# An FFT mixer and an MLP mixer in one kernel: four weight sums moved to GpSimd, and the folds of two early batches taken in other pieces at other steps

## The chip, the cores and the metric

The kernel runs on one core of a Trainium2 chip. The metric is the device time of one execution in microseconds (us); the kernel before has a median of 597.24 us over 6 executions, from 595.39 to 599.65. The engines are called by the names of the profile: PE is TensorE (PEld its weight load), DVE is VectorE, ACT is ScalarE, POOL is GpSimd, SP is SyncE.

## The reference

The input x has 8 batches of 3008 rows and 256 features. First the real part of a two-dimensional Fourier transform over rows and features is taken, then an MLP mixer: a token part over the rows and a channel part over the features, each with a relu and a residual.

```python
X = np.fft.fft(np.fft.fft(x, axis=1), axis=2).real        # (8, 3008, 256)
h = np.maximum(X.transpose(0, 2, 1) @ w_tok1, 0.0) @ w_tok2
u = X + h.transpose(0, 2, 1)
out = u + np.maximum(u @ w_ch1, 0.0) @ w_ch2              # w_ch1 256x1536, w_ch2 1536x256
```

## The kernel before

Everything is computed in f16 with f32 sums in PSUM. All loops are unrolled, and each engine works through its instructions in the order in which the program writes them; semaphores between the engines are put in from the tiles that they share. There is no planner at run time: the order is the written one, and lists of small numbers (`plan`, `own_plan`, `early_plan`, `fold_plan`) say how many pieces of a generator are taken at which place.

**Setup (lines 104 to 980)** makes the tables of the transform, loads the weights and does batch 0's transform. Loads that turn f32 into f16 are issued by POOL: x of batch 0, the token weights, `wc1` and `wc2` (the channel weights; `wc2` is tile `wc` in the profile), then x of batch 1. After the loads POOL copies most of the second token weights into aligned rows (`align_w2`, lines 976 to 978; eight copies w2p<-w2s at L305).

**A batch is 24 steps.** For each of 6 chunks `c` of 512 rows there are 4 steps `s`; step number `sub = 4 * c + s`. A step holds, in this order: three of the 12 tiles of the first channel product with relu on ACT (`mm1`, L773, L776), pieces of the batch's own transform that are still open (`own`), pieces of the next batch's transform (`nxt`), a quarter of the second channel product of the chunk before (`mm2`, L817), and block sums on DVE (`now`, `block_sums`, L790). Batch 0's step 0 starts at 32.18 us, batch 1's at 102.88.

**The second channel product** is done on 2x2 blocks with seven block products instead of eight. For that it needs sums of blocks of the activations (`block_sums`, tiles `c` and `sb`) for each chunk, and once four sums of blocks of the weights: `wst`, 128x768 each, made by `weight_sums` (lines 230 to 235) on DVE at step 3 of batch 0. Their first reader is PE in step 5 (`wst[:, 0]`, then `wst[:, 1]`), then steps 6 and 7. ACT copies partial results (`m`, L822), DVE adds them up (`osb`, L799), POOL adds the residual `rt` (L799) after filling one edge column of it (`edges`, L794), and SP issues the output. `rt` is the transposed `ut`, by DMA transposes on SP's queue (`turn_u`, L753).

**The transform of a batch** begins with `fold` on DVE (lines 451 to 474): x (`xp`) plus its mirrored rows (`xm`, loaded by an indirect gather), then even and odd parts in `eo`. It has four quarters of the 17 rows of tile, and each quarter has three pieces: add into xp (L463), even part (L467), odd part (L472). The first piece carries two short column adds more (L461, L462), the eleventh a copy and a memset (L469, L470). `front` then multiplies `eo` with tables (`inner` L518, `outer` L527, L583) into `z`, `z` into `w` (L596, L597, L599), and `w` into the token part: `tok1` (L613), `third` (L645, with ACT's `qs` L648 and DVE's two `yt` L652), and per chunk two products `pu` (L730) whose sum with `yt` DVE writes into `ut` (L738).

**Buffers.** `xp`, `xm`, `eo` have one buffer: `load_x(b)` waits until the fold of the batch before has read xp for the last time. `load_x` is four copies and two gathers on POOL (L163, L153). PSUM has three rings: tag "mm" (3 buffers, `mm1`), "o2" (2, `mm2`), "f" (3, the transform).

**What is taken where, before.** fold(1) is taken in batch 0 by `early_plan`: 2, 0, 2, 2, 3, 2, 1 pieces at steps 5 to 11; behind it at step 11 comes `load_x(2)`. fold(2) is taken by `fold_plan`: two pieces each at steps 16, 17, 20 and 21 of batch 0 and at steps 0 and 1 of batch 1; behind it at step 1 comes `load_x(3)`. fold(3) begins at step 9 of batch 1. `own_plan[1]` gives the open pieces of batch 1's transform at its own steps: first third(2), then `ut` of chunks 2 to 5 in halves.

Of the kernel before, what the change touches and what calls it, by code (L numbers as in the profile page):

```python
# [21 lines left out]
BB = 8  # L22
# [19 lines left out]
def kernel(  # L42
# [9 lines left out]
    nc = tc.nc  # L52
# [32 lines left out]
    def dram(t, offset, ap):  # L85
        return bass.AP(tensor=t, offset=offset, ap=ap)
# [8 lines left out]
    def ts(out_, in_, s1, op0, s2=None, op1=None, eng=nc.vector):  # L95
        if op1 is None:
            eng.tensor_scalar(out=out_, in0=in_, scalar1=s1, scalar2=None, op0=op0)
        else:
# [16 lines left out]
                      for n in ("tdu", "tdb", "altu"))  # L115
# [7 lines left out]
                                   in1=pcol[:], op0=AT.mult, op1=AT.add)  # L123
# [28 lines left out]
    def gather(out_, rows, index):  # L152
        nc.gpsimd.indirect_dma_start(  # L153
            out=out_, out_offset=None, in_=rows,
            in_offset=bass.IndirectOffsetOnAxis(ap=index, axis=0))

    def load_x(b):
        xp = xin.tile([KR, NR, D], FP16, tag="xp", name="xp")
        xm = xin.tile([KG, NR - 1, D], FP16, tag="xm", name="xm")
        for i in range(2):  # L160
            for q, n in ((0, 32), (32, NQ - 32)):
                p0 = i * NQ + q
                nc.gpsimd.dma_start(  # L163
                    out=xp[p0:p0 + n, :, :],
                    in_=dram(x_t, (b * S + 16 * i + 64 * q) * D,
                             [[64 * D, n], [1, NR * D]]))
        xmf = xm[:].rearrange("p t d -> p (t d)")
        for k in range(2):
            gather(xmf[:, 8 * D * k:8 * D * (k + 1)], x8, ix8[0:KG, b, k:k + 1])
        return xp, xm  # L170
# [5 lines left out]
    x_tiles = {0: load_x(0)}  # L176
# [51 lines left out]
    wst = const.tile([P, 4, HC, P], FP16, tag="wst")  # L228

    def weight_sums():  # L230
        b11, b12, b21, b22 = (wc2[:, HC * j:HC * j + HC, P * k:P * k + P]
                              for j in range(2) for k in range(2))
        for o, x, y, op in ((0, b12, b11, AT.subtract), (2, b22, b12, AT.subtract),
                            (1, wst[:, 2], b11, AT.add), (3, b21, wst[:, 1], AT.subtract)):
            nc.vector.tensor_tensor(out=wst[:, o], in0=x, in1=y, op=op)

    def swap_wc1(h):
        nc.sync.dma_start(out=wc1[1][:, h, :], in_=wc1[0][:, h, :])
# [64 lines left out]
    def copy(e, out_, in_):  # L303
        if e:
            (nc.vector, nc.gpsimd)[e - 1].tensor_copy(out=out_, in_=in_)  # L305
        else:
            nc.scalar.activation(out=out_, in_=in_, func=AFT.Copy)  # L307
# [12 lines left out]
        out=mp[:], in0=jrow[:, 0:64].unsqueeze(1).to_broadcast([P, NG, 64]),  # L320
# [123 lines left out]
    def align_w2(c, th, e):  # L444
        a = slice(8 * c, min(8 * c + 8, NQ))
        copy(e, w2p[:, th, :, a], w2v[:, th, :, a])
# [4 lines left out]
    def fold(b, engs):  # L451
        xp, xm = x_tiles.pop(b)
        eo = perb.tile([KR, NR, D], FP16, tag="eo", name="eo")
        state[b] = {"eo": eo}
        add, sub = AT.add, AT.subtract
        for s, (t0, t1) in enumerate(((13, 17), (9, 13), (5, 9), (1, 5))):
            tt = engs[s].tensor_tensor
            t = slice(t0, t1)
            rv = slice(16 - t0, 16 - t1 if t1 < 17 else None, -1)
            if s == 0:  # L460
                tt(out=xp[:, 1:NR, 0], in0=xp[:, 1:NR, 0], in1=xm[0:KR, ::-1, 0], op=add)  # L461
                tt(out=eo[:, :, 0], in0=xp[:, :, 0], in1=xp[:, :, 0], op=add)  # L462
            tt(out=xp[:, t, 1:D], in0=xp[:, t, 1:D], in1=xm[0:KR, rv, D - 1:0:-1], op=add)  # L463
            yield
            if t0 == 1:
                t = slice(0, t1)
            tt(out=eo[:, t, 1:129], in0=xp[:, t, 1:129], in1=xp[:, t, 255:127:-1], op=add)  # L467
            if t0 == 1:
                nc.vector.tensor_copy(out=nyq[:, 0:1], in_=eo[:, 0, P:P + 1])  # L469
                nc.vector.memset(eo[:, 0, P:P + 1], 0.0)  # L470
            yield
            tt(out=eo[:, t, 129:256], in0=xp[:, t, 1:128], in1=xp[:, t, 255:128:-1],  # L472
               op=sub)
            yield
# [284 lines left out]
    def plain(b, c):  # L759
        return (b, c) == (BB - 1, NCH - 1)  # L760

    def tiles(b, c):
        return 1 if c + 1 == NCH and b % 2 == 0 else 2
# [157 lines left out]
    def pair(b, c1):  # L921

        if b % 2 == 0 and b + 1 < BB:
            state["ch"] = work.tile([P, NCT, 64], FP16, tag="ch", name="ch")
            nc.vector.tensor_copy(out=state["ch"][:], in_=c1[:, :, CW - 128:CW - 64])
        elif b % 2:
            nc.vector.tensor_copy(out=c1[:, :, CW - 64:CW], in_=state["ch"][:])


    def take(g, n):  # L930
        for _ in range(n):
            next(g, None)
# [43 lines left out]
    for c in range(2, NCH):  # L976
        for th in range(2):
            align_w2(c, th, 2)
    early = fold(1, [nc.vector] * 4)
    setup.close()  # L980
    work = ctx.enter_context(tc.tile_pool(name="work", bufs=1))
# [2 lines left out]

    plan = [[0] * 10 + [2] * 10 + [1, 2, 2, 3]] + [[1] * 14 + [2, 1] * 4 + [1, 1]] * (BB - 1)
    own_plan = [[2, 1, 1, 1, 1, 1, 1, 0, 1, 1, 0, 0, 1, 1] + [0] * 10,
                [1, 1, 1, 0, 0, 1, 1, 0, 1, 1, 0, 0, 1, 1] + [0] * 10]
    own_plan += [[1, 1, 1, 0, 0, 1, 1, 0, 1, 1, 0, 0, 1, 1] + [0] * 10] * (BB - 2)
    early_plan = [0] * 5 + [2, 0, 2, 2, 3, 2, 1] + [0] * 12
    fold_plan = [[0] * 8 + [1, 2, 0, 0] * 4 for _ in range(BB)]  # L990
    fold_plan[0] = [0] * 16 + [2, 2, 0, 0, 2, 2, 0, 0]
    fold_plan[1] = [2, 2, 0, 0] + [0] * 4 + [0, 2, 0, 0] + [1, 2, 0, 0] * 2 + [2, 2, 0, 0]
    prev = None
    turned_u = {(0, 0): turn_u(0, 0)}
    for b in range(BB):
        nxt = front(b + 1) if b + 1 < BB else iter(())
        if b != 1:
            folds = fold(b + 2, [nc.vector] * 4) if b + 2 < BB else None
        for c in range(NCH):
            c1 = work.tile([P, NCT, CW], FP16, tag="c1", name="c1", bufs=2)  # L1000
            box = {"rt": turned_u.pop((b, c))}
            if not plain(b, c):
                box["sb"] = work.tile([P, 3, HC, D], FP16, tag="sb", name="sb", bufs=2)
            if c + 1 == NCH and b % 2:
                pair(b, c1)
            for s in range(4):
                sub = 4 * c + s
                n = plan[b][sub]
                mm1(b, c, c1, range(3 * s, 3 * s + 3))
                def now():  # L1010
                    which = 2 * (s % 2), 2 * (s % 2) + 1
                    if s >= 2 and not plain(b, c) and (b or c):
                        block_sums(c1, box["sb"], slice(0, 3), which, tiles(b, c))
                    elif s < 2 and prev is not None:
                        k = slice(3 if b or c > 1 else 0, HC)
                        block_sums(prev[2], pbox["sb"], k, which, tiles(*prev[0:2]))

                if s == 3:
                    now()
                take(own, own_plan[b][sub])  # L1020
                first = 0 if s % 2 else n // 2
                take(nxt, first)
                if s == 0:
                    now()
                if prev is not None:
                    mm2(*prev, s, pbox)
                if s in (1, 2):
                    now()
                take(nxt, n - first)
                if s == 2 and c + 1 < NCH:  # L1030
                    turned_u[b, c + 1] = turn_u(b, c + 1)
                if s == 3 and c + 1 == NCH and b + 1 < BB:
                    turned_u[b + 1, 0] = turn_u(b + 1, 0)
                if b == 0 and sub in (15, 17, 19, 21):
                    align_w2((sub - 15) // 4, (sub - 15) // 2 % 2, 0)
                if b == 0 and sub == 3:
                    weight_sums()
                    for h in range(2):
                        swap_wc1(h)
                if b == 0 and early_plan[sub]:  # L1040
                    take(early, early_plan[sub])
                    if sub == 11:
                        x_tiles[2] = load_x(2)
                if folds is not None and fold_plan[b][sub]:
                    take(folds, fold_plan[b][sub])
                    if b == 1 and sub == 1:
                        x_tiles[3] = load_x(3)
                        folds = fold(3, [nc.vector] * 4)
                if sub == 22 and b and b + 3 < BB:
                    x_tiles[b + 3] = load_x(b + 3)  # L1050
            if c + 1 == NCH and b % 2 == 0:
                pair(b, c1)
            prev, pbox = (b, c, c1), box
        own = nxt
# [32 lines left out]
```

## Time and profile before

| | us |
|---|---|
| median of 6 executions | 597.24 |
| the profiled execution | 596.69 |
| its span, first to last instruction | 594.9 |
| PE busy | 580.2 |
| DVE busy | 460.5 |
| ACT busy | 440.3 |
| POOL busy | 154.3 |
| PE waits listed, after 33 us | 0.2 (45.4), 0.3 (71.4), 1.2 (82.9) |
| x of batch 2: first issue, first DVE reader | 66.82, 82.07 |
| the four weight sums on DVE | 40.54 to 42.7 |

The profile is of one execution. A timeline row gives start and length in us, engine, line, operation, output <- inputs with their shapes, and in brackets how long the engine stood idle before it and for whom. A waits row gives who waited for whom, the total, the count and the longest. PE's ends are modelled; the rhythm of its starts is more exact. Intervals between starts are called pitch: an instruction overlaps the end of the one before, so a row's length is a little more than its pitch.

### The profile page before, as it was taken

How to read it: one execution, taken by the hardware profiler on the slowest of the kernel's cores; microseconds unless marked ns; L12 is line 12 of the kernel's file. 1: busy time of each engine (PE TensorE's matmuls, PEld its weight loads, DVE VectorE, ACT ScalarE, POOL GpSimd, SP SyncE). 2: the span in 40 equal slices, each digit the busy share in tenths (PEclk: the TensorE clock that was granted, in tenths of full speed). 3: DMA queues.
4: the chain of work that ended last, by engine and by line, in shares of the span. 5: the costliest groups of instructions: out<-in, count | busy, mean ns of one | idle time of the engine just before them, and what ended most of it. 6: DMA issues, size and time to landing. Idle time of an engine off the chain costs nothing.

```text
span 594.9 us, 16046 instructions
## 1 busy us (share of the span) xinstructions
PE 580.2 (98%) x6433; PEld 419.5 (71%) x6433; DVE 460.5 (77%) x1079; ACT 440.3 (74%) x997; POOL 154.3 (26%) x253
## 2 busy tenths in 40 slices
PE   5999999999999999999999999999999999999997
PEld 3846667676777677667777667766777777766676
DVE  8879788778796888769788687867888677676573
ACT  7776876877767776787777777788777877767772
POOL 7532412411242121412124211421211121112131
PEclk9999999999999999999999999999999999999999
DMA  9995591782258233653319453493343424233534
GB/s 152 211 188 126 102 131 38 140 139 54 56 114 157 54 65 81 134 91 80 83 36 180 86 77 55 81 177 57 56 68 68 80 56 94 50 72 68 86 55 105
DMA packets 86682, 56.55 MB, mean 95 GB/s; under 512 B 54944, under 2 KB 83552, under 8 KB 85856
## 3 DMA queue, kind: packets, MB, share of 16 engines
q1 hardware_dynamic: 77984, 37.77, 34.1%
q0 software_dynamic: 8320, 17.49, 17.0%
q8 instruction: 50, 0.82, 0.6%
q10 hardware_dynamic: 304, 0.26, 0.2%
q14 instruction: 24, 0.20, 0.1%
HBM read 34.98 MB, written 24.64 MB: 100 GB/s over the span
## 4 chain that ended last, share of the span: by engine, by line
PE 88%; DVE 7%; DMA 2%; issue 1%; ACT 1%; POOL 0%; DVEq 0%; POOLq 0%
PE pc L773 38%; PE px L817 23%; PE py L817 9%; PE pu L730 6%; PE pt L613 4%; DMA xm<-in_x_dram,ix 2%; DVE sb L790 1%; PE pz L518 1%; PE py L645 1%; PE pq L645 1%; PE po L888 1%; PE py L836 1%; PE pw L596 1%; PE pw L597 1%; DVE xp L463 1%
## 5 line engine op out<-in xcount | busy, mean ns | idle before, releaser
L776 ACT ACTIVATE c<-pc 128x512 f16<-128x512 f32 (+1 forms) x574 | 298.2, 596 | 26.8 <-issue 15.0
L799 POOL TENSOR_TENSOR osb<-osb,rt 128x256 f32<-128x256 f32 (+1 forms) x94 | 85.9, 913 | 385.9 <-DVE osb L799 378.8
L817 PEld LDWEIGHTS <-c 128*128 128x128 f16 x2160 | 131.1, 98 | 27.1 <-DVE c L790 1.4
L773 PE MATMUL pc<-ut,wc1p 128*128 128x512 f16 x576 | 140.0, 379 | 0.5 <-DVE ut L305 0.5
L773 PE MATMUL pc<-ut,wc1m 128*128 128x512 f16 (+1 forms) x576 | 134.9, 370 | 0.0
L822 ACT ACTIVATE m<-px 128x256 f32<-128x256 f32 (+1 forms) x141 | 52.9, 376 | 79.5 <-PE px L817 47.7
L817 PEld LDWEIGHTS <-sb 128*128 128x128 f16 x1620 | 96.8, 98 | 11.3 <-issue 0.2
L738 DVE TENSOR_TENSOR ut<-pu,yt 128x512 f16<-128x512 f32 (+1 forms) x94 | 63.2, 674 | 39.7 <-PE pu L730 39.7
L773 PEld LDWEIGHTS <-wc1p 128*128 128x128 f16 x576 | 51.9, 97 | 49.1 <-DMA wc1p<-in_moe_w_ch_dram,ixc 0.8
L773 PEld LDWEIGHTS <-wc1m 128*128 128x128 f16 x576 | 52.9, 98 | 45.0
L817 PE MATMUL px<-wst,c 128*128 128x128 f16 x1080 | 75.8, 219 | 1.2 <-DVE c L790 1.2
L817 PE MATMUL px<-wc,c 128*128 128x128 f16 x1080 | 68.0, 219 | 0.1
L799 DVE TENSOR_TENSOR osb<-py,m 128x256 f32<-128x256 f32 (+1 forms) x94 | 38.4, 408 | 25.1 <-ACT m L822 24.7
L790 DVE TENSOR_TENSOR sb<-sb,c 128x768 f16<-128x768 f16 (+2 forms) x93 | 55.1, 593 | 3.2
L730 PE MATMUL pu<-w2p,uu 128*128 128x512 f16 (+1 forms) x184 | 54.7, 379 | 0.0
L790 DVE TENSOR_TENSOR sb<-c 128x768 f16<-128x768 f16 (+2 forms) x93 | 52.0, 559 | 0.0
L790 DVE TENSOR_TENSOR c<-c 128x768 f16<-128x768 f16 (+2 forms) x93 | 51.0, 549 | 0.0
L790 DVE TENSOR_TENSOR sb<-c,sb 128x768 f16<-128x768 f16 (+2 forms) x93 | 50.9, 547 | 0.0
L307 ACT ACTIVATE z<-pz 128x480 f16<-128x480 f32 (+1 forms) x60 | 39.1, 667 | 5.5 <-PE pz L527 3.0
L599 DVE SCALAR_TENSOR_TENSOR w<-alt,pw 128x131 f16<-128x131 f16 x84 | 29.2, 351 | 16.1 <-ACT w L307 15.8
L652 DVE TENSOR_TENSOR yt<-py,qs 128x512 f16<-128x512 f32 x48 | 30.9, 686 | 10.7 <-ACT qs L648 10.5
L817 PE MATMUL px<-wst,sb 128*128 128x128 f16 x540 | 37.8, 219 | 0.3 <-DVE osb L799 0.2
(201 smaller groups left out, 637.3 us busy)
## 6 DMA issues: line engine op xcount, KB each, us to landing
out_dram<-osb SPq DMA_DIRECT2D x83, 256.0 KB, 3.4
xp<-in_x_dram POOLq DMA_DIRECT2D x16, 272.0 KB
out_dram<-osb SPq DMA_DIRECT2D x11, 192.0 KB, 3.1
xp<-in_x_dram POOLq DMA_DIRECT2D x16, 127.5 KB
rt<-ut SPq DMA_TRANSPOSE x96, 3.8
w2s<-in_moe_w_tok_dram POOLq DMA_DIRECT2D x1, 1504.0 KB
w1p<-in_moe_w_tok_dram POOLq DMA_DIRECT2D x4, 192.0 KB
wc<-in_moe_w_ch_dram POOLq DMA_DIRECT2D x1, 768.0 KB
```

The source lines that it names most:

```text
L307: nc.scalar.activation(out=out_, in_=in_, func=AFT.Copy)
L599: nc.vector.scalar_tensor_tensor(out=w[:, g, 0:131], in0=alt[:], scalar=pw[:, 131:132], in1=pw[:, 0:131], op0=AT.mult, op1=AT.add)
L613: nc.tensor.matmul(pt[:, o:o + n], lhsT=hw[:, g, th * P:th * P + P], rhs=w[:, g, f:f + n], start=(g == 0), stop=(g == NG - 1))
L652: nc.vector.tensor_tensor(out=yt[:, h, CW * c:CW * c + CW], in0=py[:], in1=qs[:], op=op)
L730: nc.tensor.matmul(pu[:, 0:n], lhsT=uu[:, th, int(minus), h, :], rhs=w2_cols(b, c)[:, th], start=(th == 0), stop=(th == 1))
L738: nc.vector.tensor_tensor(out=ut[:, h, 0:n].rearrange("p (a b) -> p a b", b=64), in0=pu[:, 0:n].rearrange("p (b a) -> p a b", b=64), in1=y ...
L773: nc.tensor.matmul(pc[:, 0:n], lhsT=wc[:, h, ct * P:(ct + 1) * P], rhs=ut[:, h, 0:n], start=(h == 0), stop=(h == 1))
L776: nc.scalar.activation(out=c1[:, ct, 0:n], in_=pc[:, 0:n], func=AFT.Relu)
L790: nc.vector.tensor_tensor(out=o, in0=x, in1=y, op=op)
L799: eng.tensor_tensor(out=o, in0=x, in1=y, op=AT.add)
L817: nc.tensor.matmul(o[:, t], lhsT=a(k)[:, f:f + P], rhs=w(k), start=(first and t == 0 and k == 0), stop=(k == HC - 1), skip_group_check=True)
L822: nc.scalar.activation(out=m[:, i, t1], in_=pa[:, 0], func=AFT.Copy)
```

## The change

`weight_sums` uses POOL instead of DVE and is called in the setup, behind POOL's copies for the row alignment, instead of at step 3 of batch 0. fold(1) is taken as 3, 1, 0, 3, 3, 2 pieces at steps 5 to 10. fold(2) is taken as three pieces each at steps 20 and 21 of batch 0 and at steps 0 and 1 of batch 1. `load_x(2)` is called at step 10 (before: 11), `load_x(3)` at step 2 of batch 1 (before: 1), and fold(3) is made there; its pieces stay at their steps. In batch 1 third(2) is taken at step 1 instead of step 0, and with it the two halves of chunk 2's `ut` at steps 2 and 4 instead of 1 and 2.

```diff
--- before.py
+++ after.py
@@ -232,7 +232,7 @@
                               for j in range(2) for k in range(2))
         for o, x, y, op in ((0, b12, b11, AT.subtract), (2, b22, b12, AT.subtract),
                             (1, wst[:, 2], b11, AT.add), (3, b21, wst[:, 1], AT.subtract)):
-            nc.vector.tensor_tensor(out=wst[:, o], in0=x, in1=y, op=op)
+            nc.gpsimd.tensor_tensor(out=wst[:, o], in0=x, in1=y, op=op)
 
     def swap_wc1(h):
         nc.sync.dma_start(out=wc1[1][:, h, :], in_=wc1[0][:, h, :])
@@ -976,6 +976,7 @@
     for c in range(2, NCH):
         for th in range(2):
             align_w2(c, th, 2)
+    weight_sums()
     early = fold(1, [nc.vector] * 4)
     setup.close()
     work = ctx.enter_context(tc.tile_pool(name="work", bufs=1))
@@ -984,12 +985,13 @@
 
     plan = [[0] * 10 + [2] * 10 + [1, 2, 2, 3]] + [[1] * 14 + [2, 1] * 4 + [1, 1]] * (BB - 1)
     own_plan = [[2, 1, 1, 1, 1, 1, 1, 0, 1, 1, 0, 0, 1, 1] + [0] * 10,
-                [1, 1, 1, 0, 0, 1, 1, 0, 1, 1, 0, 0, 1, 1] + [0] * 10]
+                [0, 1, 1, 0, 1, 1, 1, 0, 1, 1, 0, 0, 1, 1] + [0] * 10]
     own_plan += [[1, 1, 1, 0, 0, 1, 1, 0, 1, 1, 0, 0, 1, 1] + [0] * 10] * (BB - 2)
-    early_plan = [0] * 5 + [2, 0, 2, 2, 3, 2, 1] + [0] * 12
+    early_plan = [0] * 5 + [3, 1, 0, 3, 3, 2] + [0] * 13
     fold_plan = [[0] * 8 + [1, 2, 0, 0] * 4 for _ in range(BB)]
-    fold_plan[0] = [0] * 16 + [2, 2, 0, 0, 2, 2, 0, 0]
-    fold_plan[1] = [2, 2, 0, 0] + [0] * 4 + [0, 2, 0, 0] + [1, 2, 0, 0] * 2 + [2, 2, 0, 0]
+    fold_plan[0] = [0] * 20 + [3, 3, 0, 0]
+    fold_plan[1] = [3, 3] + [0] * 7 + [2] + [0, 0, 1, 2, 0, 0, 1, 2, 0, 0, 2, 2, 0, 0]
+    load_at = [10, 2]
     prev = None
     turned_u = {(0, 0): turn_u(0, 0)}
     for b in range(BB):
@@ -1034,19 +1036,17 @@
                 if b == 0 and sub in (15, 17, 19, 21):
                     align_w2((sub - 15) // 4, (sub - 15) // 2 % 2, 0)
                 if b == 0 and sub == 3:
-                    weight_sums()
                     for h in range(2):
                         swap_wc1(h)
-                if b == 0 and early_plan[sub]:
+                if b == 0:
                     take(early, early_plan[sub])
-                    if sub == 11:
-                        x_tiles[2] = load_x(2)
-                if folds is not None and fold_plan[b][sub]:
+                if folds is not None:
                     take(folds, fold_plan[b][sub])
-                    if b == 1 and sub == 1:
-                        x_tiles[3] = load_x(3)
+                if b < 2 and sub == load_at[b]:
+                    x_tiles[b + 2] = load_x(b + 2)
+                    if b:
                         folds = fold(3, [nc.vector] * 4)
-                if sub == 22 and b and b + 3 < BB:
+                if b and sub == 22 and b + 3 < BB:
                     x_tiles[b + 3] = load_x(b + 3)
             if c + 1 == NCH and b % 2 == 0:
                 pair(b, c1)
```

## The prediction

> **What bounds the kernel.** I read the page first, then who TensorE (PE) waited for, then the order of time around those waits, then the chain of waits.
>
> ```profile
> PE 580.2 (98%) x6433; PEld 419.5 (71%) x6433; DVE 460.5 (77%) x1079; ACT 440.3 (74%) x997; POOL 154.3 (26%) x253
> PEclk9999999999999999999999999999999999999999
> ```
>
> PE is busy 98% of the span at the full granted clock, so only its 594.9 − 580.2 = 14.7 us of idle time can be won. PE's waits say how little of that this change can reach:
>
> ```profile
> PE filler L294 <- DVE altu L325: 5.9, 1, 5.9
> PE px L817 <- DVE c L790: 1.2, 1, 1.2
> PE pc L773 <- DVE ut L305: 0.5, 1, 0.5
> PE pw L596 <- issue: 0.3, 1, 0.3
> PE px L817 <- DVE osb L799: 0.2, 1, 0.2
> ```
>
> The 5.9 and the 0.5 come before batch 0's first step ends and are not touched; the 0.3 (at 71.4) waits for ScalarE's copies of z. Of the work after 32 us the change can reach 1.2 + 0.2. From 84.1 us to the end no PE gap is listed at all, so time won or lost before passes whole to the end. The 1.2 us, in order of time:
>
> ```profile
> 79.82 0.35 DVE L599 SCALAR_TENSOR_TENSOR w<-alt,pw 128x131 f16<-128x131 f16 x1
> 82.07 0.23 DVE L461 TENSOR_TENSOR xp<-xp,xm 94x16 f16<-94x16 f16 x1 [1.90 <-DMA xm<-in_x_dram,ix]
> 83.16 0.43 DVE L467 TENSOR_TENSOR eo<-xp 94x512 f16<-94x512 f16 x1
> 83.50 0.55 DVE L790 TENSOR_TENSOR c<-c 128x768 f16<-128x768 f16 x1
> 84.10 0.68 PE L817 MATMUL px<-wst,c 128*128 128x128 f16 x9 [1.20 <-DVE c L790]
> ```
>
> VectorE (DVE) stood 1.90 us before the first piece of fold(2) because x2's gather had not landed; the block sums behind it in its queue came late, and PE stood 1.20. The chain of waits shows why x2 was late:
>
> ```profile
> 66.82 0.74 POOL xp L163 x2
> 70.54 11.41 DMA xm<-in_x_dram,ix
> ```
>
> GpSimd (POOL) issues the load at 66.82, once the last piece of fold(1) (65.38 to 65.86) has freed xp and POOL has ended its residual; 15.2 us later x2 is there.
>
> **The change, part by part.**
>
> *fold(2) at steps 20 and 21 instead of 16, 17, 20, 21.* Step 16 starts at 75.43, step 20 at 87.81. x2 needs 15.2 us from its first issue; even issued at 66.82 it has landed by 82.1, and the first piece is now due near 93. The 1.90 wait and PE's gap go: **−1.20**. In steps 16 and 17 DVE loses four pieces (2.5 us). What is late next? Steps 20 and 21 take three pieces each. The first three run from 82.07 to 83.50 plus 0.34: 1.8 us, where pieces 5 and 6 took 0.7 (93.00 to 93.67). They fill DVE's listed gap of 1.62 before uv at 96.30. In step 21 a full quarter is 0.60 + 0.34 + 0.34 = 1.28 against 1.06 (98.05 to 99.11): ut of chunk 0 ends 0.25 later. Its reader, step 0 of batch 1, starts at 102.88, and the second half of ut ended at 101.5: the margin of 1.37 absorbs it. **0.**
>
> *third(2) moved from step 0 to step 1 of batch 1.* Its matmuls show a small hole:
>
> ```profile
> 103.83 1.28 DVE L738 TENSOR_TENSOR ut<-pu,yt 128x512 f16<-128x512 f32 x2
> 104.18 0.39 PE L645 MATMUL pq<-tq,w 128*128 128x128 f16 x4
> 104.56 0.38 PE L645 MATMUL py<-tp,w 128*128 128x128 f16 x4
> ```
>
> Four such matmuls pitch 0.22, so py could start at 104.40; it starts at 104.56, when the DVE read of the PSUM tile before it in the ring ends (103.83 + 0.69). The same stretch of batch 3 has pq and py 0.23 apart (244.63, 244.86). A step later the tile is free: **−0.15**. On DVE its two yt (1.29) leave step 0 and meet there three pieces (1.3) instead of two. Step 1 then holds yt, block sums and pieces 10 to 12 (1.7). I walk DVE on: the sums of step 1 end near 110.3 on a PE clock where px of step 2 wants them at 110.9; ut and osb of step 2 end near 112.7, and py of step 3, which adds into the PSUM that osb reads, starts at 112.9. It holds, by 0.2 us. I charge **0 to +0.5, taken +0.2**.
>
> *x2's load at step 10, x3's at step 2.* The load still waits for the last fold(1) piece, now in step 10; by the walk below DVE gets there near 63.4 instead of 65.9. POOL issues four copies and two gathers (66.82 to 71.48, 4.7 us), now ahead of its residual of step 11, which was ready at 65.5 and comes at about 68. Behind that stand an output DMA on SyncE's queue and chunk 4's transposes (issued 69.46), whose edges are wanted only at step 20: **0**. If that cover of some 10 us were gone, it would cost the 2.5 us. x3's load waits for fold(2)'s last piece, about 112 to 113 instead of 111.6, lands 15.2 later by 128, and fold(3) begins at 132.68: **0**.
>
> *fold(1): pieces 3, 1, 0, 3, 3, 2 at steps 5 to 10 instead of 2, 0, 2, 2, 3, 2, 1 at 5 to 11.* The same 12 pieces, earlier. First reader: L518 at 58.90, which needs piece 5; six pieces had ended by 58.03. But piece 4 (0.60) now stands in step 6 ahead of step 7's sums and of the osb of 52.24 to 52.66; PE's px of step 8 began at 53.01 and needs that PSUM tile. With 0.60 more and 0.2 to 0.5 of relief, osb ends near 52.8 to 53.1, against 52.8 on a PE that runs 0.2 earlier: **0 to +0.4, taken +0.2**.
>
> *The four weight sums on POOL.* DVE loses 40.54 to 42.68, 4 × 0.55 = 2.2 us. Its next ut waits for PE's pu (41.03 + 0.59), so about 1 us is really gained: ut at 41.7, block sums at 42.3 instead of 43.26. osb, which ended at 45.54 and released px at 45.59, is early enough: **−0.23**.
>
> On POOL the four stand behind the w2p copies (30.95 to 35.36) and wait for wc. wc1p landed at 31.2 (PEld's wait), then come wc's 0.79 MB at what is POOL's part of the queues, 3.28 of 4.19 MB at about 210 GB/s in 26 to 48 us, or 0.165 MB/us: 4.8 us, **36.0**. No row shows a 128x768 sum on POOL. Nearest are its residuals with two inputs: 0.67 for 256 columns, 1.16 for 512, so 1.65 for 768 by the same slope; below it the one-input w2p copies (4.41 / 8 = 0.55 for 512, so 0.83). I take 1.65: 36.0 + 6.6 = **42.6**. PE wants the first at 44.52, the third at 45.36, the last at 49.95: hidden. On POOL only the rt edges wait behind, and they come at 45.48 when their transpose has landed.
>
> Here two pages of the Trainium skill speak against the change. "SBUF — State Buffer", § SBUF: two separate sides: GpSimd and a DVE instruction with two SBUF inputs share a port pair, and whichever starts first holds it for its whole instruction. "Perfetto Trace Analysis", § Optimizing Scalar/DVE Operations, warns that for this reason moving work between the two might not help. The trace agrees, and shows the exception:
>
> ```profile
> 45.45 0.68 DVE L738 TENSOR_TENSOR ut<-pu,yt 128x512 f16<-128x512 f32 x1
> 45.63 0.67 POOL L799 TENSOR_TENSOR osb<-osb,rt 128x256 f32<-128x256 f32 x1
> 53.14 1.21 POOL L799 TENSOR_TENSOR osb<-osb,rt 128x512 f32<-128x512 f32 x1 [6.84 <-DVE osb L799]
> 53.24 1.66 DVE L463 TENSOR_TENSOR xp<-xp,xm 94x1020 f16<-94x1020 f16 x1
> ```
>
> L463 with two SBUF inputs took 1.66 instead of 0.68 beside POOL; L738 with one input in PSUM kept its 0.68. From 36.0 to 42.3 DVE runs only ts, yt and ut, all with a PSUM input. By the bare rule I would charge 6.6 us of stopped DVE; by the rows only the first block sum waits, 42.3 to 42.6, and is still ahead of today's 43.26: **0**.
>
> **Sum.** −1.20 − 0.15 − 0.23 + 0.2 + 0.2 = −1.2. The profiled execution took 596.69 (span 594.9 and 1.8 around it), so 595.5 for its like. It lies 0.55 below the median of 597.24; from the median, **596.0**. Executions of the kernel before spread over 4.3 us, so about 0.5% (3 us) is what a measurement of it can tell from no change.
>
> **Rivals.**
> - *The waits only move* (the change doesn't do what it says): DVE is 9 tenths busy from 40 to 66 and again from 86 to 115, and the two tight places above (py of step 3, px of step 8) take 0.5 and 0.4, with 0.3 more as px of step 4 meets a late osb. For it: DVE has hardly a listed gap there. Against: each margin was positive in my walk. −1.58 + 1.2 = −0.4: 596.9.
> - *All gains, no new wait*: −1.6, and up to 0.3 more at 71.4: 595.4. For it: PE's rhythm of batch 3 without the hole. It cannot win much more, since no more idle time is there.
> - *Slower: POOL's sums hold the shared port.* Place: 42.3 to 50 us. If a sum took P instead of 1.65, the block sums (DVE, two SBUF inputs) would wait until 36.0 + 4P when POOL keeps taking the pair first. From P = 1.8 that is later than today's 43.26; at P = 3 it is 48.0, PE loses 4.7, and 597.24 − 1.4 + 4.7 = 600.5. For it: the 1.66 row. Against: P = 3 is almost twice the row's slope.
>
> **How the numbers follow.** Likeliest case 0.53 (596.0, own range 594.3 to 597.7 with the scatter of a median), waits move 0.22 (596.9), all gains 0.10 (595.4), slower 0.15 (598 to 604). All but the last lie within 0.5% of 597.24, that is 594.25 to 600.2. Scatter gives 0.08 to faster from the first and third; of the slower case 0.12 lies beyond. The range, 593.5 to 600.3, leaves out most of the slow case and the tails.
>
> **What would show it.** Right: no xm wait on DVE before fold(2) and no gap at px L817 near 83; POOL rows of L235 near 36 to 43 at about 1.65; DVE's L790 at about 42.6; PE busy still 580, span near 593.7. Wrong: L235 on POOL over 2 us or starting after 38; new PE waits for DVE osb near 53 or 112, or for wst; a later rt.

## The result, and the profile after

The changed kernel takes **594.41 us** in the median of 32 executions (594.20 to 596.50); the kernel before, over 69 executions that include the six shown above, 597.04 us (595.12 to 601.22). The ratio is 0.9957, with an interval of [0.9945, 0.9968]: 2.6 us or 0.4% faster. The forecast was 596.0 (593.5 to 600.3): direction and place were right, and the gain was twice the size. The profiled execution took 594.41, its span 592.6, against 596.69 and 594.9.

The page, and the waits of PE over the whole span (who waited for whom, total, count, longest). Of the waits in the first 33 us only the two are shown that the prediction shows too:

```profile
PE 580.5 (98%) x6433; PEld 420.1 (71%) x6433; DVE 460.7 (78%) x1075; ACT 439.8 (74%) x997; POOL 162.5 (27%) x257
...
PEclk9999999999999999999999999999999999999999
```

```profile
PE filler L294 <- DVE altu L325: 5.9, 1, 5.9
...
PE pc L773 <- DVE ut L305: 0.5, 1, 0.5
...
PE px L817 <- DVE osb L799: 0.4, 1, 0.4
```

PE has the same busy time (580.5 against 580.2), and the span has become shorter by 2.3: all of the gain is idle time of PE. The wait for `c` (1.2) and the two small ones at 45.4 and 71.4 are gone from the list; one of 0.4 is new. Next the order of time at each place that the prediction named:

```profile
36.04 3.25 POOL L235 TENSOR_TENSOR wst<-wc 128x768 f16<-128x768 f16 x2 [0.41 <-DMA wc<-in_moe_w_ch_dram]
39.37 1.64 POOL L235 TENSOR_TENSOR wst<-wst,wc 128x768 f16<-128x768 f16 x1
41.08 1.64 POOL L235 TENSOR_TENSOR wst<-wc,wst 128x768 f16<-128x768 f16 x1
...
41.76 0.69 DVE L738 TENSOR_TENSOR ut<-pu,yt 128x512 f16<-128x512 f32 x1 [1.03 <-PE pu L730]
42.36 1.17 DVE L790 TENSOR_TENSOR sb<-c 128x1536 f16<-128x1536 f16 x1
...
51.38 0.68 DVE L463 TENSOR_TENSOR xp<-xp,xm 94x1020 f16<-94x1020 f16 x1
...
52.92 0.41 DVE L799 TENSOR_TENSOR osb<-px,rt 128x256 f32<-128x256 f32 x1
...
53.38 0.83 PE L817 MATMUL px<-wc,c 128*128 128x128 f16 x12 [0.37 <-DVE osb L799]
...
63.99 2.13 POOL L163 DMA_DIRECT2D xp<-in_x_dram  x4 [6.56 <-DVE eo L472]
...
82.29 0.83 PE L817 MATMUL px<-wst,c 128*128 128x128 f16 x12
...
90.88 0.22 DVE L461 TENSOR_TENSOR xp<-xp,xm 94x16 f16<-94x16 f16 x1
...
104.24 0.39 PE L645 MATMUL pq<-tq,w 128*128 128x128 f16 x4
104.46 0.39 PE L645 MATMUL py<-tp,w 128*128 128x128 f16 x4
```

The four sums run on POOL from 36.04 to 42.72. DVE's first block sum starts at 42.36, meets the last of them and takes 1.17 instead of 0.95; it ends at 43.53, where before it ended at 44.21. Piece 4 of fold(1), the add at 51.38 that is now taken in step 6, pushes `osb` to 52.92 (before: 52.24), and PE stands for it in step 8, at 53.38. x2 is asked for at 63.99 instead of 66.82; the first piece of fold(2) comes at 90.88 with no wait, and the twelve matmuls of step 18 run through where there was a hole of 1.20. `py` of third(2) follows `pq` by 0.22 instead of 0.38.

The wait list is reckoned from PE's modelled ends, and understates the holes: the one listed as 1.20 is 1.37 by the starts. Here is the same comparison from PE's starts: how much longer than its usual pitch (0.055 for these 128-column matmuls) each interval is, and so how far each later step has moved against before, counted from batch 0's step 0:

| place | predicted | moved by |
|---|---|---|
| px of step 5 (weight sums gone from DVE) | −0.23 | −0.39 |
| py of step 7, new | 0 | +0.14 |
| px of step 8 (piece 4 ahead of osb) | +0.2 | +0.53 |
| small holes at steps 9, 10 to 12, 14, 20 | 0 | −0.19 −0.16 −0.30 −0.25 |
| px of step 18 (x2 late) | −1.20 | −1.60 |
| py of third(2) | −0.15 | −0.16 |
| py of step 3 of batch 1 | +0.2 | 0 |
| sum | −1.2 | −2.4 |

Step 0 itself starts 0.10 later after the change, which leaves the 2.3 of the spans.

Two rows of this pair are in part accident, and nearly cancel. The −0.30 of step 14 (the wait at 71.4) is missing in every other profiled execution of this study, also where only fold(2) or only third(2) was moved and all instructions up to there are those of the kernel before; so its loss is not the work of the change. And in those two executions PE stands 0.22 longer at step 9 than in the profiled one of before, so that the change is worth about 0.4 there instead of 0.19.

### The profile page after: what moved, and what is told of

It is laid out like the page before. It is cut to its first block, busy times and chain, and to the rows that moved or that the text cites. A ratio compares the mean times of both kernels' runs of the same rounds, so it can differ in the third digit from the quotient of the medians.

```text
span 592.6 us, 16047 instructions
## 1 busy us (share of the span) xinstructions
PE 580.5 (98%) x6433; PEld 420.1 (71%) x6433; DVE 460.7 (78%) x1075; ACT 439.8 (74%) x997; POOL 162.5 (27%) x257
## 4 chain that ended last, share of the span: by engine, by line
PE 94%; DVE 4%; ACT 1%; issue 0%; DVEq 0%; POOL 0%; POOLq 0%
PE pc L773 40%; PE px L817 25%; PE py L817 10%; PE pu L730 7%; PE pt L613 4%; PE pz L518 2%; PE pq L645 1%; PE py L645 1%; PE po L888 1%; PE py L836 1%; PE pw L596 1%; DVE sb L790 1%; PE pw L597 1%; PE pw L560 0%; ACT z L307 0%
## 5 line engine op out<-in xcount | busy, mean ns | idle before, releaser
L776 ACT ACTIVATE c<-pc 128x512 f16<-128x512 f32 (+1 forms) x574 | 298.6, 598 | 26.8 <-issue 15.2
L652 DVE TENSOR_TENSOR yt<-py,qs 128x512 f16<-128x512 f32 x48 | 30.9, 686 | 10.4 <-ACT qs L648 10.2
L817 PE MATMUL py<-wst,sb 128*128 128x128 f16 x540 | 37.9, 219 | 0.0
```

Of the source, the lines that this page charges most:

```text
L652: nc.vector.tensor_tensor(out=yt[:, h, CW * c:CW * c + CW], in0=py[:], in1=qs[:], op=op)
L776: nc.scalar.activation(out=c1[:, ct, 0:n], in_=pc[:, 0:n], func=AFT.Relu)
L817: nc.tensor.matmul(o[:, t], lhsT=a(k)[:, f:f + P], rhs=w(k), start=(first and t == 0 and k == 0), stop=(k == HC - 1), skip_group_check=True)
```

## The experiments

Rows are compared with the profiled execution of the kernel before; "moved" is always by PE's starts, as in the table. Executions of the kernel before on the three chips of these runs number 89, with a median of 597.55.

### One part of the change alone

**Only the weight sums on POOL.** From the kernel before:

```diff
-            nc.vector.tensor_tensor(out=wst[:, o], in0=x, in1=y, op=op)
+            nc.gpsimd.tensor_tensor(out=wst[:, o], in0=x, in1=y, op=op)
...
             align_w2(c, th, 2)
+    weight_sums()
...
-                    weight_sums()
```

> The kernel before with only the four weight sums moved to POOL behind the row alignment. My theory (the large gain comes from fold(2) leaving steps 16 and 17): PE's late start of px in step 5 (0.39 by its pitch) goes, perhaps also 0.2 in step 9; the first issue of x2's load comes at most 1 us earlier than 66.82, so DVE still waits for xm near 82 and PE keeps at least 1.0 of its 1.6 in step 18. In all -0.4 to -1.1 us, 596.3. Rival (2.2 us less on DVE is the gain): the chain through DVE to x2's load moves 2.2 us earlier, the wait for xm is gone, and the kernel is 2 us or more faster, 595.0.

Measured: 597.11 (595.68 to 601.50), ratio 0.9994 [0.9962, 1.0026]. No slower, so the rival in which POOL's sums stop DVE falls for this size; and no faster that could be measured. x2's load was expected up to 1 us earlier; it came 0.4 later. In the profiled execution (598.9) `wc` landed late, the last sum ended at 43.45, and the first block sum was held until then (42.41, 1.86 long), so that PE's px of step 5 gained only 0.08. That execution also showed something not expected. POOL's issue of x2, DVE's wait for it, and PE behind it:

```profile
67.25 2.13 POOL L163 DMA_DIRECT2D xp<-in_x_dram  x4
...
82.94 0.23 DVE L461 TENSOR_TENSOR xp<-xp,xm 94x16 f16<-94x16 f16 x1 [2.65 <-DMA xm<-in_x_dram,ix]
...
84.97 0.68 PE L817 MATMUL px<-wst,c 128*128 128x128 f16 x9 [1.95 <-DVE c L790]
```

and its windows (from:to, length, then busy us and instructions of PE, PEld, DVE, ACT, POOL; then PE's granted clock, DMA share, GB/s):

```profile
83.50:85.50 2.00, 0.53 (x9) 0.53 (x10) 1.97 (x5) 0.62 (x2) 0.00 (x0) 1.00 1.82 252
85.50:87.50 2.00, 1.95 (x10) 0.79 (x8) 2.00 (x7) 1.22 (x4) 0.00 (x0) 0.65 0.37 72
87.50:89.50 2.00, 2.00 (x16) 1.56 (x15) 1.97 (x5) 1.17 (x2) 0.00 (x0) 0.50 0.00 0
89.50:91.50 2.00, 2.00 (x24) 1.45 (x23) 1.78 (x6) 1.07 (x4) 0.68 (x1) 1.00 0.00 0
```

x2 was asked for 0.4 us later than before and landed 0.9 later. PE's hole grew from 1.20 to 1.95, and behind it the granted clock fell to one half: 0.65 in one window is a half clock for 1.4 us of it, and with the next window's 2.0 that makes 3.4 us, in which PE does 1.7 us of work. So 0.4 us in the load's issue came with 0.75 more of hole and 1.7 of lost clock.

**Only fold(2) later:**

```diff
-    fold_plan[0] = [0] * 16 + [2, 2, 0, 0, 2, 2, 0, 0]
-    fold_plan[1] = [2, 2, 0, 0] + [0] * 4 + [0, 2, 0, 0] + [1, 2, 0, 0] * 2 + [2, 2, 0, 0]
+    fold_plan[0] = [0] * 20 + [3, 3, 0, 0]
+    fold_plan[1] = [3, 3] + [0] * 7 + [2] + [0, 0, 1, 2, 0, 0, 1, 2, 0, 0, 2, 2, 0, 0]
```

> The kernel before with only fold(2) moved: three pieces each at steps 20 and 21 of batch 0 and steps 0 and 1 of batch 1; sums on DVE, fold(1), loads and third(2) as before. My theory: the stall in step 18 (1.6 by pitch) and a late px in step 20 (0.26) go, nothing comes back before step 0 of batch 1; there third(2) still waits for its PSUM tile (0.16, up to 0.5 with three pieces on DVE). In all -1.5 to -1.9 us, 595.4. Rival (the moves need each other; three pieces at a time on a DVE without the relief of the sums make new waits at steps 20 to 25): at most -0.8.

Measured: 595.15 (594.86 to 595.51), ratio 0.9946 [0.9926, 0.9966]; moved −1.50. The hole of step 18 is gone, and so is the spread: 0.65 us over ten executions, where before spreads over 6. Up to step 21 it had won 1.9; 0.39 went again in batch 1, where third(2) at step 0 now stands beside three pieces instead of two: its `py` waits 0.36 in all for DVE, and a `px` at step 4 waits 0.20 for `osb`. This one part holds most of the gain.

**Only fold(1) earlier, with x2's load at step 10:**

```diff
-    early_plan = [0] * 5 + [2, 0, 2, 2, 3, 2, 1] + [0] * 12
+    early_plan = [0] * 5 + [3, 1, 0, 3, 3, 2] + [0] * 13
...
-                    if sub == 11:
+                    if sub == 10:
```

> The kernel before with only fold(1) taken as 3, 1, 0, 3, 3, 2 pieces and x2's load at step 10. My theory: px of step 8 waits for osb behind piece 4 and py of step 7 behind piece 3, 0.7 to 1.1 us lost; the load is issued near 64.5, lands near 79.7, the wait for xm goes and with it most of the 1.6 in step 18. In all -0.4 to -1.0, so an earlier load and a later fold are two cures of one stall. Rival (DVE without the relief ends fold(1) no earlier than before): the load is not earlier by more than 1 us, the stall stays over 1 us, and the kernel is 0 to 1 us slower.

Measured: 595.29 (595.07 to 596.85), ratio 0.9955 [0.9936, 0.9975]; moved −1.17. x2 was issued at 65.98, in an execution whose step 0 began 1.35 later than before, and DVE did not wait for it; py of step 7 and px of step 8 lost 0.47 and 0.54. An earlier load and a later reader are two cures of the same stall: each of them takes it away alone, and so together they cannot bring the sum of both.

**Only third(2) one step later:**

```diff
-                [1, 1, 1, 0, 0, 1, 1, 0, 1, 1, 0, 0, 1, 1] + [0] * 10]
+                [0, 1, 1, 0, 1, 1, 1, 0, 1, 1, 0, 0, 1, 1] + [0] * 10]
```

> The kernel before with only third(2) of batch 1 moved from step 0 to step 1 and chunk 2's halves behind it. My theory: py of third(2) no longer waits for its PSUM tile, -0.16; step 18 and all before step 24 is unchanged. Rival (the later ut of chunk 2 or yt beside fold pieces delays PE): 0 to +0.5 in steps 1 to 4 of batch 1.

Measured: 597.15 (595.68 to 600.69), ratio 0.9995 [0.9966, 1.0023]. The row moved by −0.16 at py, as predicted, and nothing else did that the edit explains. In its profiled execution (595.68) x2 happened to land so that DVE waited 0.85 instead of 1.90, and the hole of step 18 was 0.53 instead of 1.60, with the same instructions up to there. The stall is not a constant.

### What the spread says

Each execution has its own mean granted clock. Half a clock for 3.4 us of 597 gives a mean of 0.997. Of the 89 executions of the kernel before, 36 show 0.997 or less, with a median of 599.56 (598.53 to 602.64); the 53 others have a median of 596.75 (595.17 to 598.90). Of the 20 executions of the two kernels that leave x2's load and fold(2) as they were (sums alone, third(2) alone), 7 are of that kind. Of the 82 executions of the other kernels of this study in which the load is earlier or fold(2) later, and POOL has no extra work, not one is, nor any of the changed kernel. So the tail of the kernel before comes from the late x2. That the fall of the clock sits at step 18 was seen in the profiled execution above; in the others it is inferred from the size and from what removes it.

Another source of scatter lies ahead of step 0. In the profiled executions with fold(1) alone earlier, and with piece 4 at step 7 (below), PE waited 0.90 and 1.05 in the setup for the first token weights (`w1p`, `w1m`), and step 0 began 1.35 and 1.19 late. "Moved" leaves this out, the times don't. Whether it is what makes the changed kernel's 594.20 to 596.50 was not seen.

### One part of the change undone

**The changed kernel with the sums on DVE again** (engine and place as before):

```diff
-            nc.gpsimd.tensor_tensor(out=wst[:, o], in0=x, in1=y, op=op)
+            nc.vector.tensor_tensor(out=wst[:, o], in0=x, in1=y, op=op)
...
-    weight_sums()
...
+                    weight_sums()
```

> The changed kernel with the four weight sums back on DVE at step 3; all else as changed. My theory: the sums are a small part. px of step 5 is late again by 0.39 and py of step 7 by 0.5 instead of 0.14, together 0.6 to 1.0 us over the changed kernel: 595.2. x2 is issued near 66 and still lands before step 20, so no stall at step 18, times as narrow as those of the changed kernel and no half clock. Rival (the relief of DVE is what made room for the others): 596.5 or more, with waits at steps 20 to 25 that the changed kernel has not.

Measured: 595.07 (594.59 to 596.28), ratio 0.9954 [0.9928, 0.9981]; moved −1.96. px of step 5 shows its 0.39 again; the 0.5 expected at py of step 7 did not come (+0.18 against before). By the rows the sums are worth 0.4, by the medians 0.66; the two ratios to the kernel before (0.9954 and 0.9957) can't tell them apart.

**The changed kernel with fold(1) and x2's load as before:**

```diff
-    early_plan = [0] * 5 + [3, 1, 0, 3, 3, 2] + [0] * 13
+    early_plan = [0] * 5 + [2, 0, 2, 2, 3, 2, 1] + [0] * 12
...
-    load_at = [10, 2]
+    load_at = [11, 2]
```

> The changed kernel with fold(1) taken as before (2, 0, 2, 2, 3, 2, 1) and x2's load at step 11 again. My theory: the earlier load is not needed once fold(2) begins at step 20: no stall at step 18. The wait of px at step 8 (0.53) goes, one at step 9 (0.2 to 0.4) comes back: 594.0 to 594.4. Rival (the earlier load is what cured the stall): 1 us or more of it stays, 595.5, and times scatter as those of the kernel before.

Measured: 594.23 (593.95 to 595.19), ratio 0.9939 [0.9916, 0.9963]. No stall at step 18: fold(2)'s move is enough. The earlier fold(1) costs the 0.14 and 0.53 of steps 7 and 8 and buys back 0.35 at step 9 and 0.17 at step 12, which stand again here; so by the rows it costs 0.15 on balance. In the profiled execution `wc` landed at 37.3, POOL's sums ended at 44.74 and px of step 5 stood 0.72, so its shift (−1.81) is no fair measure of the edit.

**The changed kernel with piece 4 at step 7 instead of 6:**

```diff
-    early_plan = [0] * 5 + [3, 1, 0, 3, 3, 2] + [0] * 13
+    early_plan = [0] * 5 + [3, 0, 1, 3, 3, 2] + [0] * 13
```

> The changed kernel with piece 4 of fold(1) at step 7 instead of step 6 (3, 0, 1, 3, 3, 2). My theory: px of step 8 no longer waits for osb behind that piece (0.53), at most 0.2 comes back at step 9: 593.9 to 594.2, faster than the changed kernel by 0.3 to 0.5 us. Rival (the wait at step 8 is DVE's whole load in steps 5 to 7 and not this piece): no change, or the same 0.5 one step later.

Measured: 594.92 (593.76 to 595.49), ratio 0.9941 [0.9920, 0.9962]; moved −2.46. The wait of px at step 8 is gone, which shows that piece 4 made it, but py of step 7 stands 0.45 in its place, and px of step 5 0.13 behind a late `wc` (first sum at 37.63). The 0.3 to 0.5 that were expected of it don't show in the median, and the medians don't separate the two orders.

### The port, and the late load

**Four more sums on POOL**, into a tile that nobody reads, behind the four of the changed kernel:

```diff
+    spare = const.tile([P, HC, P], FP16, tag="spare")
...
+        for _ in range(4):
+            nc.gpsimd.tensor_tensor(out=spare[:], in0=b12, in1=b11, op=AT.subtract)
```

> The changed kernel with four more sums of the same shape on POOL behind the four, into a tile that nobody reads (work added, nothing left out): POOL is busy with them from about 42.7 to 49.3. If POOL keeps taking the port pair first, as in my slower rival: DVE's block sums stand until 49, PE loses 4 to 5 us, and its clock may be halved as well, 599 to 602. If DVE gets the pair at the end of each POOL instruction: each two-input DVE instruction waits at most 1.65, three or four do so, PE loses 1.5 to 3.5 us: 596 to 598. If DVE is not held by POOL at all: no change, 594.4.

Measured: 601.22 (598.87 to 602.89), ratio 1.0055 [1.0031, 1.0079]. Order of time on both engines (line numbers are three higher here), then PE's waits:

```profile
42.24 1.75 DVE L793 TENSOR_TENSOR sb<-c 128x1536 f16<-128x1536 f16 x1
44.03 2.28 DVE L793 TENSOR_TENSOR sb<-sb,c 128x1536 f16<-128x1536 f16 x1
46.23 0.41 DVE L802 TENSOR_TENSOR osb<-px,m 128x256 f32<-128x256 f32 x1
...
50.85 1.66 DVE L464 TENSOR_TENSOR xp<-xp,xm 94x16 f16<-94x16 f16 x1
...
43.14 9.29 POOL L238 TENSOR_TENSOR spare<-wc 128x768 f16<-128x768 f16 x4
```

```profile
PE py L820 <- DVE osb L802: 3.7, 1, 3.7
PE px L820 <- DVE osb L802: 1.4, 1, 1.4
```

Here DVE really is held by POOL, as in the slower rival of the prediction. From 42 us until POOL is done, every DVE instruction with two inputs in SBUF waits for one of POOL's, even one of 16 columns (1.66; 0.22 alone in the changed kernel), and POOL's take 2.2 to 2.4 each instead of 1.64: the two engines take turns. By its time (599 to 602) the theory in which POOL keeps the port would have been right; by the rows it is the second one, which had been put at 596 to 598. `osb`, with an input in PSUM, keeps its 0.41. PE stood 5.1 us in all, and the clock was halved for 6.8 us from within the hole of 3.7; in step 8 PE was 7.7 behind the kernel before, at the end 5.1. The price of being held was understated: the fall of the clock comes on top.

**The kernel before with x2's load one step later:**

```diff
-                    if sub == 11:
-                        x_tiles[2] = load_x(2)
+                if b == 0 and sub == 12:
+                    x_tiles[2] = load_x(2)
```

> The kernel before with x2's load called at the end of step 12 instead of 11; all else as before. My theory: the load is issued behind POOL's edges and residual of step 12, near 69 to 70 instead of 66.8, so x2 lands 2 to 3 us later, PE's stall in step 18 grows from 1.6 to about 4 us by pitch, and PE's clock is halved for 3.4 us behind it in nearly every execution, which costs 1.7 more: 599.5 to 602, and no execution under 597. Rival (x2's landing doesn't set the kernel's time and its scatter; the clock is halved by something else): about 597 to 598, with the scatter of the kernel before.

**The changed kernel with that load at step 12:**

```diff
-    load_at = [10, 2]
+    load_at = [12, 2]
```

> The changed kernel with x2's load called at the end of step 12 instead of 10: the same delay where fold(2) begins at step 20. My theory: x2 lands by about 85, its first reader comes near 91: no stall, no half clock, 594.2 to 594.6 as the changed kernel. Rival (the earlier load is what cured the stall): 596 or more, and scatter.

Measured: 608.98 (607.13 to 609.51, four executions), ratio 1.0179 [1.0122, 1.0235], and 595.24 (594.26 to 596.67), ratio 0.9958 [0.9930, 0.9986]. Issue and first reader, with PE's wait, of the first:

```profile
69.28 2.12 POOL L163 DMA_DIRECT2D xp<-in_x_dram  x4
...
93.32 0.23 DVE L461 TENSOR_TENSOR xp<-xp,xm 94x16 f16<-94x16 f16 x1 [13.10 <-DMA xm<-in_x_dram,ix]
```

```profile
PE px L817 <- DVE c L790: 12.4, 1, 12.4
```

and of the second:

```profile
68.81 2.12 POOL L163 DMA_DIRECT2D xp<-in_x_dram  x4
...
91.34 0.23 DVE L461 TENSOR_TENSOR xp<-xp,xm 94x16 f16<-94x16 f16 x1 [0.23 <-DMA xm<-in_x_dram,ix]
```

The direction is as expected: the load's time decides where fold(2) is due early, and is hidden where it is due late. Neither size is. In the first, 2.5 us later in issue became 11.2 later in landing. The median of the second is 0.8 above the changed kernel; by the starts 0.3 of it is a longer wait of py at step 7, the rest is not explained.

Why the load took so long can be read, in part, from the other profiled executions. SP issues chunk 4's transposes (`rt`) near the load: in the kernel before, in the changed kernel, and in the kernel before with the load at step 12:

```profile
69.46 6.91 SPq L753 DMA_TRANSPOSE rt<-ut  x2
...
71.54 4.08 SPq L753 DMA_TRANSPOSE rt<-ut  x2
...
69.38 3.41 SPq L753 DMA_TRANSPOSE rt<-ut  x2
```

The load's two gathers took this long to land with fold(1) alone (load at step 10), the sums alone (step 11) and the load at step 12:

```profile
DMA to landing us min/median/max: 7.3/7.6/8.0
...
DMA to landing us min/median/max: 11.8/11.8/11.8
...
DMA to landing us min/median/max: 19.4/19.8/20.2
```

Over all profiled executions in which the last gather's landing is recorded, both counted from the load's first issue:

| load called at | transposes issued after | last gather landed after |
|---|---|---|
| step 10 (six executions) | 7.5 to 8.0 | 12.0 to 12.2 |
| step 11 (four) | 1.5 to 2.3 | 13.8 to 17.1 |
| step 12 (the two above) | 0.1 | 23.9, 22.4 |

A load that is out well ahead of the transposes takes 12 us, and one that is issued with them nearly twice that. The transposes lose too: those of chunk 4 took 12.9 and 12.1 us to land in the kernel before, and 6.0 and 3.7 in the changed kernel. That the transposes are the cause fits all of this, but they were not moved alone. For x2 it means that a call at step 10 pays twice, in issue and in landing. With fold(2) at step 20 its first reader comes about 15 us after the landing with the load at step 10, 6.9 and 9.6 us after it with the load at step 11, and with the load at step 12 DVE waits 0.23.

### A version with one sum back on DVE

In the changed kernel DVE stands 1.03 before `ut` at 41.76, and the next block sum then waits for POOL's last sum. One weight sum fits into that hole.

**One sum on DVE at step 3, three on POOL, piece 4 at step 7:**

```diff
-    def weight_sums():
+    def weight_sums(eng, which):
...
-                            (1, wst[:, 2], b11, AT.add), (3, b21, wst[:, 1], AT.subtract)):
-            nc.gpsimd.tensor_tensor(out=wst[:, o], in0=x, in1=y, op=op)
+                            (1, wst[:, 2], b11, AT.add),
+                            (3, b21, wst[:, 1], AT.subtract))[which]:
+            eng.tensor_tensor(out=wst[:, o], in0=x, in1=y, op=op)
...
-    weight_sums()
+    weight_sums(nc.gpsimd, slice(1, 4))
...
+                    weight_sums(nc.vector, slice(0, 1))
...
-    early_plan = [0] * 5 + [3, 1, 0, 3, 3, 2] + [0] * 13
+    early_plan = [0] * 5 + [3, 0, 1, 3, 3, 2] + [0] * 13
```

> The changed kernel with the first of the four weight sums on DVE at step 3, where DVE stands idle for about 1 us, the other three on POOL, and fold(1) as 3, 0, 1, 3, 3, 2. My theory: POOL's last sum ends before DVE's first block sum also where wc lands late, so the port is free; px of step 5 is on time (0.39 to 0.74 saved against the late cases), px of step 8 does not wait, py of step 7 waits 0.1 to 0.5: 593.8 to 594.1, 0.3 to 0.6 below the changed kernel. Rival (DVE's sum waits for POOL's port or for its writes and delays ut): 594.5 or more.

**The same with 2, 1, 1, 3, 3, 2 pieces at steps 5 to 10:**

> As the kernel with the split sums, but fold(1) as 2, 1, 1, 3, 3, 2: piece 3 at step 6 instead of 5. My theory: the osb that py of step 7 waits for is 0.34 earlier, so that wait goes (0.1 to 0.5); px of step 8 has piece 3 ahead of it instead of piece 4 and waits at most 0.2: 593.6 to 594.0. Rival (the wait only moves to step 8): no gain over the other.

Measured: **593.79** (593.70 to 594.81), ratio 0.9934 [0.9911, 0.9957], and 594.19 (593.63 to 594.61), ratio 0.9939 [0.9915, 0.9963]. Of the first:

```profile
39.62 1.64 POOL L236 TENSOR_TENSOR wst<-wc,wst 128x768 f16<-128x768 f16 x1
...
40.65 1.02 DVE L236 TENSOR_TENSOR wst<-wc 128x768 f16<-128x768 f16 x1
41.77 0.69 DVE L739 TENSOR_TENSOR ut<-pu,yt 128x512 f16<-128x512 f32 x1
42.37 0.95 DVE L791 TENSOR_TENSOR sb<-c 128x1536 f16<-128x1536 f16 x1
```

POOL is done at 41.26; DVE's sum is held by its last one (1.02 instead of 0.56) and still ends before `ut` can start; the block sum is not held. No PE wait after 33 us is listed any more, and by the starts one of 0.15 is left (py of step 7). The span is 592.1. Against the changed kernel's 594.41 that is 0.6 us. Ten of the twelve executions lie below the fastest of the changed kernel's 32 (594.20), but the two were not measured together and their intervals overlap: faster than the changed kernel is likely, not shown. With 2, 1, 1 the wait comes back in parts: 0.16 at step 7, 0.27 at step 8, 0.23 at step 10.

## Why the prediction was half right

**Right: where the gain is.** fold(2) behind the load takes away the wait for x2 and PE's hole at step 18; done alone it gave 0.9946. No other wait took its place: steps 20 and 21 of batch 0 absorbed three pieces each.

**Right: POOL's sums are hidden.** 36.04 to 42.72 against 36.0 to 42.6 predicted, 1.64 each against 1.65, and only the first block sum met them. The exclusive port of the Trainium skill's page "SBUF — State Buffer", § SBUF: two separate sides, is real in this kernel, as the four more sums show, but the work that DVE does at that time has an input in PSUM (`c`, `yt` and `ut`; the prediction's `ts` is a misreading of `c<-pc`, without effect). The rule as the prediction quotes it covers only DVE instructions with two SBUF inputs, so the 6.6 us "by the bare rule" were never due by it. The margin is thin: it hangs on when `wc` lands (POOL's first sum starts at 36.0 to 37.6 in these runs), and with a start at 37.3 px of step 5 stood 0.72, more than the 0.39 that moving the sums had won.

**Right in place, off in size: px of step 5, step 8 and third(2).** −0.39, +0.53 and −0.16 were taken as −0.23, +0.2 and −0.15. The py of step 3 in batch 1, charged at +0.2, cost 0. The new waits came to 0.67 instead of 0.4, and a wait for `osb` near 53 was even named as a sign of being wrong; the gain elsewhere covered it. third(2)'s move seems worth more than the hole it closes: fold(2) alone lost 0.39 in batch 1, the changed kernel nothing. The changed kernel without that move was not run.

**Wrong: the size of the term of step 18, −1.20**, and with it the statements that the change can reach 1.2 + 0.2 us of PE's idle time and that a case without new waits "cannot win much more" than 595.4. Three things were in it.
- The list of waits was taken for the idle time. By PE's starts the hole was 1.37, and 0.22 more behind the next matmuls: 1.6. Four more places with holes of 0.16 to 0.30 are in no list, or only in part, and went too (that of step 14 by accident). That makes −2.4 in the pair of profiled executions instead of −1.2.
- The hole was taken for a constant. In the three profiled kernels that leave the load and fold(2) where they were it was 0.53 (third(2) alone), 1.6 (before) and 2.3 us (sums alone), as x2 landed. The fastest execution of each kernel, 595.12 and 594.20, lie only 0.92 apart, about what the rows other than step 18 add up to (−0.8); that the rest of the gain is x2's landing is inferred from this and from the spread.
- The prediction noted that the profiled execution lay 0.55 below the median and that executions spread over 4.3 us, and carried −1.2 over to the median unchanged. The spread was part of what the change acts on. In 36 of 89 executions the mean clock tells of at least one half-clock stretch of 3.4 us, which moves their median by 0.8 (597.55 over all, 596.75 without these). With 2.3 from the profiled pair this makes about 3.1, an estimate, where the medians give 2.6 over the executions that stand behind the ratio and 3.1 against those 89.

**Right, and for more than was thought: x2's load ahead of the transposes.** It was charged 0, because the later transposes are wanted only at step 20. They were issued 2.1 us later (71.54 against 69.46) and yet landed earlier (the first at 77.51 against 82.36). The load itself took 12 us in all six like executions with a recorded landing, where the prediction carried over 15.2.

## What to carry to other kernels

Measure a stall from the starts of the waiting engine, not from the list of waits alone, and look at the spread of the executions before sizing a fix: a transfer without margin shows up as a wide, slow tail, and the fix is worth the tail too. Between an earlier transfer and a later reader one is enough; take the one that costs less at its new place. When a transfer is moved, look at what is issued beside it, since its own duration can change more than its start. Sums with two SBUF inputs were nearly free on GpSimd here because what VectorE did meanwhile read PSUM; four more of them were not. And a single profiled execution has accidents: a hole counts for a change only if it stands in other executions of the same instructions too.

## What was not expected of the hardware

- **The clock falls after a short hole.** The Trainium skill's page "TensorE: Matmul & The Clock Gate" puts the half rate behind an idle window of about 3.4 us (Part 1, The HAM clock gate) and advises against gaps of more than about 3 us (§ Why this matters for your kernels). Here a hole of 1.95 us (2.1 by the starts) was followed by a half clock for 3.4 us, which began about 1 us after PE had resumed, while holes of 1.20 and 1.4 (1.4 and 1.5 by the starts) were not. In the two other profiled executions with such a fall it began within the hole (3.7 and 12.4 us) and lasted 6.8 and 10.2 us, two and three times as long. The length of the slow stretch agrees with the page; the length of the hole doesn't. How much idle time is enough can't be told from three falls.
- **DVE and POOL take turns on the port.** With both queues full neither starves: each of five DVE instructions with two SBUF inputs waited for one of POOL's, and POOL's took 2.2 to 2.4 instead of 1.64.
- **The same load took 12.0 to 23.9 us** from its first issue to the landing of its last gather, by how near to the transposes it was issued.
